# Two decode layers over a KV cache: layer 1's loop behind the kept heads, one K tile loaded in between, their results copied by ScalarE

## The chip, the cores and the metric

The kernel runs on one core of one Trainium2 chip. The metric is the device time of one execution in microseconds (us). A core has five engines with a queue each: TensorE (PE; its weight loads are listed as PEld), VectorE (DVE), ScalarE (ACT), GpSimd (POOL) and SyncE (SP), and 16 DMA engines that they share. All data is in HBM at the start; it has to be brought into SBUF, the core's working memory, before an engine can use it. Matrix products land in PSUM.

## The reference

Two equal layers, each an attention block with a KV cache of 16,384 positions, followed by a small mixer and MLP. One new token for each of two batches; 32 heads of width 128, model width 576, MLP width 4608; bf16 inputs.

```python
def _A_ref(x, k_cache, v_cache, wq, wo):
    q = (x @ wq).reshape(B, Sq, H, Dh).transpose(0, 2, 1, 3)
    scores = jnp.einsum("bhqd,bhkd->bhqk", q, k_cache) * (Dh ** -0.5)
    p = _softmax(scores, axis=-1)
    o = jnp.einsum("bhqk,bhkd->bhqd", p, v_cache)
    return o.transpose(0, 2, 1, 3).reshape(B, Sq, H * Dh) @ wo
...
x = x + _A_ref(_layernorm(x), A_k_cache, A_v_cache, A_wq, A_wo)
x = x + _B_ref(_layernorm(x), B_w1, B_w2, B_w3, B_w4)
x = x + _A_ref(_layernorm(x), A_k_cache, A_v_cache, A_wq, A_wo)
x = x + _B_ref(_layernorm(x), B_w1, B_w2, B_w3, B_w4)
```

Both layers read the same caches, 2 x 32 heads with 4.19 MB of K and 4.19 MB of V each, and the same weights.

## The kernel before, in words

**Work and order.** One step of a layer is one (batch, head) with its K tile and V tile, each 128 partitions x 128 rows of 128 numbers. There are U = 64 steps in each layer. Layer 0 takes the heads in order; layer 1 starts with the last three (`order`), whose tiles are still in SBUF when layer 0 ends, so that these need not be loaded again: heads 62 and 63 whole (`CARRY = 2`), of head 61 the K tile and the last 56 of 128 rows of V; the other `GONE = 72` rows give their place to weights and are loaded again in four pieces.

**Memory and loads.** `mem` has six slots of one tile each. `plan_all` writes down by hand the list of all loads with their places; `Store.pump` issues them on SP strictly in that order, each as soon as its place is free. A tile is free when the last instruction that reads it is done, so SP waits for TensorE, VectorE or ScalarE, and behind a waiting load all later loads wait too. In the loops two V tiles of neighbouring heads come as one load of 8.39 MB, a pair (`plan_pair`).

**One step.** Half of a K tile's rows (64 of each partition's 128) go over TensorE: eight chunks, each of eight transposes into PSUM (`transposes`, L1297), an evacuation by ScalarE (`evacuate`, L1313) and eight matmuls with the query (`scores`, L1327). The other half goes over VectorE: four times a product with the query copied to all partitions (L1347) and a sum (L1353, `dots`). `q_broadcast` makes the next step's query (L1261 to L1271: two VectorE instructions, one matmul, one ScalarE copy). `softmax_max` takes the maxima on VectorE and the maximum over partitions on GpSimd (L1369); `softmax_exp` is on ScalarE (L1378 to L1384); `pv` is 128 matmuls with V (L1468). In the loops `pv_pair` does two heads with 256 matmuls (L1442), after `spread_p` (L1416, L1422), and ScalarE copies the two results (L1446).

**Loops.** In each layer most steps are a loop of two steps a turn, with the instructions of TensorE, ScalarE and VectorE written once: steps `ENTER` to `LEAVE`, 1 to 61 in layer 0 and 4 to 62 in layer 1. What stands ahead of the loop and behind it is straight code. GpSimd has no loop: it tells the looped engines of each tile that has landed (`landed`, a wait and an increment in GpSimd's order) and does the maxima in between.

**Between the layers.** Behind layer 0's attention come the projections with wo, w3 and w4, then wq for layer 1. The weights pass through small places in slots 1 and 4. TensorE meanwhile transposes the kept heads' other half (`turn`), since layer 1 takes heads 62 and 63 over TensorE alone. `carried` then is steps 0, 1 and 2 of layer 1, written out by hand: scores of both kept heads (`still`), the rest of head 61's K (`fresh`, `third`, `dots`), and the three softmaxes and V products. Step 3 (and, behind the loop, steps 62 and 63) run in the same straight loop body as in layer 0. In the version before, step 3 stands between `carried` and the loop, and the V product of step 2 runs inside it.

**Results.** Each head's output column goes to `o_acc` and its sum to `l`: for steps outside the loops by VectorE (`keep_o`, `keep_l`), inside by ScalarE.

Of the kernel before, what the change touches and what calls it, by code (L numbers as in the profile page):

```python
# [328 lines left out]
class KB:  # L329
# [183 lines left out]
    def plan_all(self):  # L513
# [37 lines left out]

        first = self.order(1)[self.CARRY + 1]
# [6 lines left out]
        assert a == self.CARRY + 2 and z == U - 2  # L559
# [10 lines left out]
        self.cuts["wo", 1] = [(i, j, 3 * T + i * row) for i, j in ((0, 11), (11, 22), (22, 32))]  # L570
        at = 3 * T + 32 * row
        ats = [at, at + w3r, at + 2 * w3r, T, T + w3r]
        assert at + 3 * w3r <= 5 * T
        w4_at = T + w3r + w3r // 2
        self.cuts["w4", 1] = [(a, b, w4_at + a * row) for a, b in ((0, 8), (8, 16))] + \
                             [(a, b, 5 * T + (a - 16) * row) for a, b in ((16, 26), (26, 30), (30, 34), (34, 36))]
        w1_at = 5 * T + 20 * row
        assert w4_at + 16 * row <= 2 * T and w1_at + 5 * row <= 6 * T
        self.plan_rows("wo", 1, self.wo, self.cuts["wo", 1])
# [394 lines left out]
    def attention(self, l):  # L974
# [11 lines left out]
        for s in range(self.CARRY + 1 if l else 0, U):  # L986
# [11 lines left out]
            if s == enter + 1:  # L998
                self.pool(lambda e: e.memset(self.both[64:, 0, :], 0.0), writes=[*self.both_keys, "cleared"])
            after = self.early(l, s - 1)  # L1000
            for c in range(2 * n):
# [16 lines left out]
                if after:  # L1018
                    if c == 2:
                        self.softmax_max(l, s - 1, o[s - 1])  # L1020
                        self.keep_o(l, s - 2)
                        self.keep_l(l, s - 2)
                        self.softmax_exp(l, s - 1, o[s - 1])
                        self.landed(l, "v", o[s - 1])
                    if c in (4, 5):
                        self.pv(l, s - 1, o[s - 1], 2 * c - 8)
                        self.pv(l, s - 1, o[s - 1], 2 * c - 7)
                elif turning:
# [11 lines left out]
                if s >= leave:  # L1040
                    if c == n and still and s == U - self.CARRY:
                        self.unturned = [(v, b) for v in o[U - self.CARRY:] for h in range(2)
                                         for b in range(h * self.BP + self.PB, (h + 1) * self.BP, self.CH)]
                        self.unsettled, self.full = [], ()
                    if c == n and still and (s < U - 1):
                        self.turn(4)
                    if s > leave and (l or s < U - 1):
                        if c == n:
                            self.softmax_exp(l, s - 1, o[s - 1])
                            if l == 0 and s == U - self.CARRY:  # L1050
                                self.store.carve(("v", o[s - 1], 0, self.NB), [self.GONE // 4 * i for i in (1, 2, 3, 4)])
                            self.landed(l, "v", o[s - 1])
                        if 0 <= c - n < 4:
                            self.pv(l, s - 1, o[s - 1], c - n)
            if turning:
# [11 lines left out]
            elif s == enter - 1:  # L1067
                while pend:
                    self.scores(*pend.pop(0))
                self.softmax_max(l, s, u)  # L1070
                if s - 1 >= 0:
                    self.keep_o(l, s - 1)
                    self.keep_l(l, s - 1)
                self.softmax_exp(l, s, u)
                self.landed(l, "v", u)
                self.keep_pair_l(l, s)
                for g in range(4):
                    self.pv(l, s, u, g)
                at = self.place(l, s)
                self.act(lambda e, at=at: e.activation(out=self.o_acc[:, at:at + 1], in_=self.mps[:, 448:449], func=ACT.Copy),  # L1080
                         reads=["ops"], writes=["o_acc"])
        if l == 0:
# [75 lines left out]
    def carried(self, o):  # L1158
# [31 lines left out]
        still(1, 0, N)  # L1190
        self.q_broadcast(o[3], 3)
        self.softmax_exp(1, 0, o[0])
# [65 lines left out]

    def q_broadcast(self, u, s):
        i = self.ix(self.l_now, s)  # L1260
        self.dv(lambda e, c: e.tensor_copy(out=self.q_col[:, i:i + 1], in_=self.q_f[:, bass.ds(c, 1)]),  # L1261
                reads=["q_f"], writes=[("q_col", i)], sig=("qc", i), col=u)
# [4 lines left out]
        qps = self.sps[i][:, 256:384]  # L1267
        self.pe(lambda pe: pe.matmul(qps, lhsT=self.ones_bf[:, :], rhs=self.diag[:, :],  # L1268
                                     start=True, stop=True, skip_group_check=True),
                reads=["ones_bf", "diag"], writes=[("qps", i)], sig=("q", i))  # L1270
        self.act(lambda e: e.activation(out=self.qb[i][:, :], in_=qps, func=ACT.Copy),  # L1271
                 reads=[("qps", i)], writes=[("qb", i)], sig=("qb", i))

# [115 lines left out]
    def keep_o(self, l, s):  # L1389

        self.dv(lambda e, c: e.tensor_copy(out=self.o_acc[:, bass.ds(c, 1)], in_=self.mps[:, 448:449]),
                reads=["ops"], writes=["o_acc"], sig="keep_o", col=self.place(l, s))

# [31 lines left out]
    def keep_pair_l(self, l, s):  # L1425
# [4 lines left out]
                 reads=[("ls0", i), ("ls1", i)], writes=["l"], sig=("keep_l", i), col=self.place(l, s))  # L1430

    def pv_pair(self, l, s, u):

# [16 lines left out]
    def pv(self, l, s, u, g):  # L1450
# [12 lines left out]
        def f(pe):  # L1463
            for b0, m, _, buf, _ in runs:
                for j in range(m):
                    b = b0 + j
                    col = self.column(l, s, b)
                    ins = pe.matmul(self.mps[:, 448:449], lhsT=buf[:, j * 128:(j + 1) * 128], rhs=p[:, col:col + 1],  # L1468
                                    start=b == 0, stop=b == self.NB - 1, skip_group_check=True)
# [98 lines left out]
```

## Time and profile before

| | |
|---|---|
| median of 3 runs | 2552.99 us (2551.66 to 2553.33) |
| profiled execution: its own time | 2552.08 us |
| profiled execution: span from first to last instruction | 2550.1 us |
| mean granted TensorE clock | 0.619 |
| busy: PE, DVE, ACT, POOL | 1588.0, 1875.4, 1250.1, 106.0 us |
| DMA queue of the loads | 1092.39 MB, 99.7% of 16 engines' span |

A busy time says how long an engine was occupied, not whether anyone waited for it. Where an instruction's row ends in brackets, its engine stood idle before it for so many us, and what the brackets name ended that; "issue" is time in which the engine waited for nothing that the profile shows. Rows of SP are the issues of loads, not the loads themselves: "x2" holds two issues, the first at the start and the second at the end of the time given. Line numbers are those of the version before.

### The profile page before, as it was taken

How to read it: one execution, taken by the hardware profiler on the slowest of the kernel's cores; microseconds unless marked ns; L12 is line 12 of the kernel's file. 1: busy time of each engine (PE TensorE's matmuls, PEld its weight loads, DVE VectorE, ACT ScalarE, POOL GpSimd, SP SyncE). 2: the span in 40 equal slices, each digit the busy share in tenths (PEclk: the TensorE clock that was granted, in tenths of full speed). 3: DMA queues.
4: the chain of work that ended last, by engine and by line, in shares of the span. 5: the costliest groups of instructions: out<-in, count | busy, mean ns of one | idle time of the engine just before them, and what ended most of it. 6: DMA issues, size and time to landing. Idle time of an engine off the chain costs nothing.

```text
span 2550.1 us, 75502 instructions
## 1 busy us (share of the span) xinstructions
PE 1588.0 (62%) x34642; PEld 1521.6 (60%) x34642; DVE 1875.4 (74%) x1815; ACT 1250.1 (49%) x2110; POOL 106.0 (4%) x154
## 2 busy tenths in 40 slices
PE   4556666566566566566776666566566566665666
PEld 3556656566565565565766566565565565565665
DVE  5787787777877877877748777877877877777775
ACT  3454555554554544544534544544544545555543
POOL 0000000000000000000000000000000000000000
PEclk8666566665656666665656666665665666656655
DMA  9999999999999999999999999999999999999999
GB/s 411 428 435 432 430 437 431 431 438 429 432 436 428 432 438 428 434 435 428 412 415 389 419 435 431 433 435 429 435 436 428 440 432 427 434 438 426 432 432 395
DMA packets 38431, 1093.18 MB, mean 429 GB/s; under 512 B 4196, under 2 KB 5352, under 8 KB 11496
## 3 DMA queue, kind: packets, MB, share of 16 engines
q1 hardware_dynamic: 38376, 1092.39, 99.7%
q8 instruction: 41, 0.67, 0.1%
q14 instruction: 14, 0.11, 0.0%
HBM read 1092.37 MB, written 0.00 MB: 428 GB/s over the span
## 4 chain that ended last, share of the span: by engine, by line
DMA 59%; DVE 26%; PE 7%; issue 5%; ACT 2%; SPq 0%; POOL 0%; POOLq 0%; DVEq 0%; ACTq 0%
DMA mem<-in_A_k_cache_dram 57%; DVE s_dve L1353 16%; DVE prod L1347 9%; PE tps L1297 3%; DMA mem<-in_B_w_dram 1%; PE mps L1468 1%; PE sps L1327 1%; PE mps L1442 1%; ACT kt L1313 1%; PE sps L1268 1%; SPq L101 0%; ACT mem L1313 0%; DVE diag L1264 0%; DVE q_col L1261 0%; DMA mem<-in_A_wq_dram 0%
## 5 line engine op out<-in xcount | busy, mean ns | idle before, releaser
L1353 DVE TENSOR_REDUCE s_dve<-prod 128x16 f32<-128x2048 bf16 x504 | 1151.2, 2284 | 13.2
L1313 ACT ACTIVATE kt<-tps 128x1024 bf16<-128x1024 bf16 x992 | 965.9, 1029 | 183.2 <-PE tps L1297 172.0
L1347 DVE TENSOR_TENSOR prod<-mem,qb 128x2048 bf16<-128x2048 bf16 x492 | 602.2, 1224 | 533.3 <-POOLq L202 482.9
L1297 PE MATMUL tps<-same,mem 128*128 128x128 bf16 x8192 | 911.4, 285 | 34.0 <-issue 26.4
L1297 PEld LDWEIGHTS tps<-same,mem 128*128 128x128 bf16 x8192 | 732.2, 131 | 40.1 <-issue 32.3
L1442 PEld LDWEIGHTS mps<-both,mem 128*128 128x128 bf16 x15104 | 407.6, 103 | 47.6 <-ACT both L1422 43.3
L1442 PE MATMUL mps<-both,mem 128*128 128x2 bf16 x15104 | 412.6, 165 | 32.0 <-ACT both L1422 27.8
L1327 PE MATMUL sps<-q_col,kt 128*128 128x1 bf16 x7936 | 364.2, 168 | 50.5 <-ACT kt L1313 45.2
L1327 PEld LDWEIGHTS sps<-q_col,kt 128*128 128x128 bf16 x7936 | 351.9, 108 | 69.4 <-ACT kt L1313 67.1
L1416 PE MATMUL sps<-p,same 128*128 128x128 bf16 x236 | 46.6, 301 | 484.3 <-ACT p L1384 484.3
L1416 PEld LDWEIGHTS sps<-p,same 128*128 128x128 bf16 x236 | 15.5, 110 | 494.3 <-ACT p L1384 494.3
L1268 PE MATMUL sps<-diag,same 128*128 128x128 bf16 x126 | 36.1, 286 | 286.6 <-DVE diag L1264 281.3
L1369 POOL PARTITION_ALL_REDUCE mx<-mx x128 | 102.9, 804 | 2374.6 <-DVE mx L1367 2257.1
L1446 ACT ACTIVATE o_acc<-mps 128x2 f32 x59 | 10.2, 173 | 382.9 <-PE mps L1442 382.9
L1378 ACT ACTIVATE mx<-mx 128x1 f32<-128x1 f32 x128 | 26.0, 203 | 337.7 <-POOL mx L1369 337.7
L1268 PEld LDWEIGHTS sps<-diag,same 128*128 128x128 bf16 x126 | 13.2, 105 | 296.6 <-DVE diag L1264 296.6
L1271 ACT ACTIVATE qb<-sps 128x128 bf16<-128x128 f32 x123 | 33.9, 275 | 219.6 <-PE sps L1268 219.6
L1422 ACT ACTIVATE both<-sps 64x256 bf16<-64x256 f32 x118 | 44.5, 378 | 57.5 <-PE sps L1416 57.5
L1364 DVE TENSOR_REDUCE mx<-sps 128x1 f32<-128x64 f32 x128 | 28.2, 220 | 24.9 <-PE sps L1327 24.8
L1381 ACT ACTIVATE p<-s_dve,mx 128x64 bf16<-128x64 f32 x123 | 42.8, 348 | 4.0
L1313 ACT ACTIVATE mem<-tps 128x1024 bf16<-128x1024 bf16 x32 | 31.6, 1030 | 20.9 <-PE tps L1297 18.0
L1428 ACT ACTIVATE l<-ls 128x1 f32 (+1 forms) x120 | 35.4, 295 | 9.2
(131 smaller groups left out, 460.6 us busy)
## 6 DMA issues: line engine op xcount, KB each, us to landing
mem<-in_A_k_cache_dram SPq DMA_DIRECT2D x124, 4096.0 KB, 24.6
mem<-in_A_v_cache_dram SPq DMA_DIRECT2D x5, 4096.0 KB, 32.0
mem<-in_B_w_dram SPq DMA_DIRECT2D x21, 576.0 KB, 8.0
mem<-in_B_w_dram SPq DMA_DIRECT2D x7, 1152.0 KB, 40.9
mem<-in_A_v_cache_dram SPq DMA_DIRECT2D x3, 2048.0 KB, 39.0
mem<-in_A_wq_dram SPq DMA_DIRECT2D x10, 512.0 KB, 7.0
mem<-in_A_wo_dram SPq DMA_DIRECT2D x8, 576.0 KB, 16.4
mem<-in_A_wq_dram SPq DMA_DIRECT2D x4, 1024.0 KB, 8.1
```

What stands on the lines that cost most here:

```text
L1268: self.pe(lambda pe: pe.matmul(qps, lhsT=self.ones_bf[:, :], rhs=self.diag[:, :], start=True, stop=True, skip_group_check=True), reads=["o ...
L1297: ins = pe.transpose(self.tps[t][:, j * 128:(j + 1) * 128], buf[:, j * 128:(j + 1) * 128], self.ident[:, :])
L1313: self.act(lambda e: e.activation(out=out, in_=self.tps[t][:, :], func=ACT.Copy), reads=[("tps", t)], writes=keys, sig=("evac", c, t, k))
L1327: ins = pe.matmul(self.sps[sp][:, c * self.CH + j:c * self.CH + j + 1], lhsT=buf[:, j * 128:(j + 1) * 128], rhs=self.q_col[:, sp:sp + 1], ...
L1347: self.dv(lambda e: e.tensor_tensor(out=prod, in0=buf.rearrange("p (j d) -> p j d", d=128), in1=qbc, op=ALU.mult), reads=[("qb", r)] + key ...
L1353: self.dv(lambda e: e.tensor_reduce(out=sd[:, c0:c0 + DB], in_=prod, axis=AX.X, op=ALU.add), reads=["prod"], writes=[("s_dve", r)], sig=(" ...
L1369: self.pool(lambda e: e.partition_all_reduce(mx[3], mx[2], channels=128, reduce_op=ROP.max), reads=[("mx2", i), "cleared"], writes=[("mx3" ...
L1381: self.act(lambda e: e.activation(out=p[:, n:self.NB], in_=self.s_dve[i][:, 0:self.NB - n], func=ACT.Exp, bias=mx[4], scale=self.scale, ac ...
L1416: ins = pe.matmul(out[:, h * n:(h + 1) * n], lhsT=lhsT, rhs=self.p[i][:, :], start=True, stop=True, skip_group_check=True)
L1422: self.act(lambda e: e.activation(out=self.both[lo:hi, k, :], in_=out[lo:hi, :], func=ACT.Copy), reads=[("sps", 0), ("qps", 0)], writes=se ...
L1428: self.act(lambda e, c: e.activation(out=self.l[:, bass.ds(c, 1)], in_=self.ls[:, 0, i:i + 1], func=ACT.Identity, bias=self.ls[:, 1, i:i + ...
L1442: ins = pe.matmul(self.mps[:, 448:450], lhsT=buf[:, b * 128:(b + 1) * 128], rhs=self.both[:, :, col], start=b == 0, stop=b == 2 * self.NB ...
```

## The change

The loop of layer 1 takes steps 3 to 61 instead of 4 to 62, so that `carried` is directly followed by the loop, and three steps instead of two come behind it. The places in `mem` and the order of loads change with it: K of step 3 comes in four pieces into slot 3, K of step 4 into slot 5, then K of step 61, one of the last heads, into slot 0, where it stays until the loop is over; pairs go to slots 1 and 2. V of step 3 is loaded as half of a pair. In `carried` the V products come one after the other instead of in halves between the chunks, step 2's as well, and `keep_by_act` lets ScalarE copy the three results. Step 3's query is spread through PSUM bank 0. Behind the loops, `softmax_max` of the step before stands one chunk earlier, ahead of the second of VectorE's four products, and `softmax_exp` stands at chunk 2 instead of chunk 4; in layer 0 the four transposes of `turn(4)`, which stood at chunk 4, come behind all chunks of step 62.

```diff
-    ENTER = (1, 4)
-    LEAVE = (61, 62)
+    ENTER = (1, 3)
+    LEAVE = (61, 61)
...
-        for i in (1, 2, 3, None, 0):
-            if i is None:
-                self.plan_piece("k", first, T, self.rows_of("k", first), 0, quarter)
-            else:
-                self.plan_piece("v", third, 4 * T, self.rows_of("v", third), i * self.GONE // 4, self.GONE // 4)
+        for i in (1, 2, 3, 0):
+            self.plan_piece("v", third, 4 * T, self.rows_of("v", third), i * self.GONE // 4, self.GONE // 4)
...
-        self.plan_tile("k", first, 3, (quarter, half, half + quarter), quarter)
-        self.plan_tile("v", first, 5)
         for s in range(a, z, 2):
-            self.plan_tile("k", o[s], 0)
-            self.plan_tile("k", o[s + 1], 2)
-            self.plan_pair(o[s], 3)
-        self.plan_tile("k", o[z], 1)
-        self.plan_tile("k", o[z + 1], 5)
-        self.plan_tile("v", o[z], 0)
-        self.plan_tile("v", o[z + 1], 2, (half,))
+            self.plan_tile("k", o[s], 3, (quarter, half, half + quarter) if s == a else ())
+            self.plan_tile("k", o[s + 1], 5)
+            if s == a:
+                self.plan_tile("k", o[z], 0)
+            self.plan_pair(o[s], 1)
+        self.plan_tile("k", o[z + 1], 4)
+        self.plan_tile("k", o[z + 2], 3)
+        self.plan_tile("v", o[z], 5)
+        self.plan_tile("v", o[z + 1], 1)
+        self.plan_tile("v", o[z + 2], 2, (half,))
...
                 elif s > leave:
-                    if c == LEAD:
+                    if c == LEAD - 1:
                         self.softmax_max(l, s - 1, o[s - 1])
...
-                    if c == n and still and (s < U - 1):
-                        self.turn(4)
-                    if s > leave and (l or s < U - 1):
-                        if c == n:
-                            self.softmax_exp(l, s - 1, o[s - 1])
...
+                if s > leave and (l or s < U - 1):
+                    if c == LEAD:
+                        self.softmax_exp(l, s - 1, o[s - 1])
...
+            if still and s == U - self.CARRY:
...
+                self.turn(4)
...
-        self.q_broadcast(o[3], 3)
+        self.q_broadcast(o[3], 3, 0)
...
-        for g in range(2):
+        for g in range(4):
             self.pv(1, 0, o[0], g)
+        self.keep_by_act(1, 0)
         third(3)
         fresh(5)
-        for g in range(2, 4):
-            self.pv(1, 0, o[0], g)
         third(4)
         fresh(6)
+        dots(2)
         self.softmax_exp(1, 1, o[1])
-        dots(2)
-        self.keep_o(1, 0)
-        self.keep_l(1, 0)
         third(5)
         fresh(7)
-        for g in range(2):
-            self.pv(1, 1, o[1], g)
         third(6)
-        for g in range(2, 4):
-            self.pv(1, 1, o[1], g)
         third(7)
         dots(3)
+        self.softmax_max(1, 2, o[2])
+        for g in range(4):
+            self.pv(1, 1, o[1], g)
+        self.softmax_exp(1, 2, o[2])
+        self.keep_by_act(1, 1)
+        self.landed(1, "v", o[2])
+        for g in range(4):
+            self.pv(1, 2, o[2], g)
+        self.keep_by_act(1, 2)
...
+    def keep_by_act(self, l, s):
+
+        i, c, k = self.ix(l, s), self.place(l, s), 448
+        self.act(lambda e: e.activation(out=self.o_acc[:, c:c + 1], in_=self.mps[:, k:k + 1], func=ACT.Copy),
+                 reads=["ops"], writes=["o_acc"])
+        if self.columns(l, s) == self.NB:
+            self.act(lambda e: e.activation(out=self.l[:, c:c + 1], in_=self.ls[:, 0, i:i + 1], func=ACT.Copy),
+                     reads=[("ls0", i)], writes=["l"])
+        else:
+            self.keep_pair_l(l, s)
```

The last weights of layer 1 move to other slots with the tiles: wo to slots 4 and 5, w3 to slots 4, 5 and 0, w4 to slots 0 and 3, w1 to slot 3 (before: 3 and 4; 3, 4 and 1; 1 and 5; 5).

More of the change, by code (lines that the diff above doesn't have):

```diff
@@ new lines, in plan_all @@
+            self.plan_pair(o[s], 1)
[4 more added lines that the diff above has]
+        self.plan_tile("v", o[z + 2], 2, (half,))
+        self.cuts["wo", 1] = [(i, j, 4 * T + i * row) for i, j in ((0, 11), (11, 22), (22, 32))]
+        at = 4 * T + 32 * row
+        ats = [at, at + w3r, at + 2 * w3r, 0, w3r]
+        assert at + 3 * w3r <= 6 * T
+        w4_at = w3r + w3r // 2
@@ L575, in plan_all @@
         self.cuts["w4", 1] = [(a, b, w4_at + a * row) for a, b in ((0, 8), (8, 16))] + \
-                             [(a, b, 5 * T + (a - 16) * row) for a, b in ((16, 26), (26, 30), (30, 34), (34, 36))]
-        w1_at = 5 * T + 20 * row
-        assert w4_at + 16 * row <= 2 * T and w1_at + 5 * row <= 6 * T
+                             [(a, b, 3 * T + (a - 16) * row) for a, b in ((16, 26), (26, 30), (30, 34), (34, 36))]
+        w1_at = 3 * T + 20 * row
+        assert w4_at + 16 * row <= T and w1_at + 5 * row <= 4 * T
@@ L1039, in attention @@
                             self.keep_l(l, s - 2)
[L1040 to L1044, printed above, removed]
-                    if c == n and still and (s < U - 1):
-                        self.turn(4)
-                    if s > leave and (l or s < U - 1):
-                        if c == n:
[L1049 to L1054, printed above, removed]
+                if s > leave and (l or s < U - 1):
+                    if c == LEAD:
+                        self.softmax_exp(l, s - 1, o[s - 1])
+                        if l == 0:
+                            self.store.carve(("v", o[s - 1], 0, self.NB), [self.GONE // 4 * i for i in (1, 2, 3, 4)])
+                        self.landed(l, "v", o[s - 1])
+                    if 0 <= c - n < 4:
+                        self.pv(l, s - 1, o[s - 1], c - n)
+            if still and s == U - self.CARRY:
+                self.unturned = [(v, b) for v in o[U - self.CARRY:] for h in range(2)
+                                 for b in range(h * self.BP + self.PB, (h + 1) * self.BP, self.CH)]
+                self.unsettled, self.full = [], ()
+                self.turn(4)
             if turning:
@@ L1389, in keep_o @@
     def keep_o(self, l, s):
-        self.dv(lambda e, c: e.tensor_copy(out=self.o_acc[:, bass.ds(c, 1)], in_=self.mps[:, 448:449]),
-                reads=["ops"], writes=["o_acc"], sig="keep_o", col=self.place(l, s))
+        k, c = 448, self.place(l, s)
+        self.dv(lambda e: e.tensor_copy(out=self.o_acc[:, c:c + 1], in_=self.mps[:, k:k + 1]),
+                reads=["ops"], writes=["o_acc"])
     def keep_l(self, l, s):
```

41 lines of the change are left out of this document (11 added, 30 removed).

## The prediction

> **What bounds the kernel now.** I read the page first, then the windows (columns: busy us of PE, PEld, DVE, ACT, POOL; PEclk; DMA share; GB/s), then the timelines of single engines around the places that the change touches.
>
> ```profile
> span 2550.1 us, 75502 instructions
> HBM read 1092.37 MB, written 0.00 MB: 428 GB/s over the span
> DMA 59%; DVE 26%; PE 7%; issue 5%; ACT 2%; SPq 0%; POOL 0%; POOLq 0%; DVEq 0%; ACTq 0%
> 1525.00:2378.14 853.14, 530.23 (x11399) 509.69 (x11398) 644.31 (x573) 427.90 (x727) 35.27 (x44) 0.62 1.00 433
> 1370.00:1412.00 42.00, 29.14 (x650) 26.21 (x648) 32.49 (x28) 25.58 (x42) 1.60 (x2) 0.75 0.85 346
> ```
>
> The kernel is a stream of 1092 MB. In the loop the DMA share is 1.00 at 433 GB/s, so a 4.19 MB tile takes 9.7 us and a turn of four tiles 38.8 us, and no engine is busy for more than 644 of 853 us. The change leaves the bytes as they are, so it can only win where the stream runs dry, or lose where it makes it dry. The second window is the one dry place of any size: (433 − 346) / 433 × 42 us = 8.4 us, right behind the entry into layer 1's loop. That is the ceiling of the gain. Finer windows and the issues on SP show why:
>
> ```profile
> 1382.00:1384.00 2.00, 0.50 (x5) 0.50 (x6) 1.97 (x2) 1.00 (x6) 0.45 (x1) 0.50 1.06 459
> 1384.00:1386.00 2.00, 2.00 (x32) 1.92 (x29) 1.97 (x5) 1.48 (x3) 0.00 (x0) 0.50 0.42 180
> 1386.00:1388.00 2.00, 1.54 (x26) 1.44 (x25) 2.00 (x2) 1.77 (x3) 0.00 (x0) 0.69 0.00 0
> 1388.00:1390.00 2.00, 0.35 (x8) 0.27 (x8) 1.07 (x5) 0.63 (x3) 0.35 (x1) 1.00 1.04 270
> 1398.00:1400.00 2.00, 0.34 (x13) 0.28 (x11) 1.97 (x2) 0.00 (x0) 0.00 (x0) 0.50 0.21 82
> 1400.00:1402.00 2.00, 1.36 (x17) 1.27 (x17) 1.97 (x5) 0.17 (x1) 0.00 (x0) 0.50 1.11 360
> 1402.00:1404.00 2.00, 2.00 (x27) 2.00 (x26) 2.00 (x1) 1.96 (x3) 0.00 (x0) 0.50 0.46 164
> 1321.75 0.33 SPq L101 DMA_DIRECT2D mem<-in_A_v_cache_dram  x1
> 1329.41 10.80 SPq L101 DMA_DIRECT2D mem<-in_A_k_cache_dram  x2
> 1353.02 0.33 SPq L101 DMA_DIRECT2D mem<-in_A_v_cache_dram  x1
> 1372.85 14.95 SPq L101 DMA_DIRECT2D mem<-in_A_k_cache_dram  x2
> 1400.76 0.33 SPq L101 DMA_DIRECT2D mem<-in_A_v_cache_dram  x1
> ```
>
> The row 1372.85 holds two issues, the second at its end, 1387.5. The queue empties at 1384.9 (180 of 433 GB/s in that slice), because the K tile of 1372.85 is the last that was issued; the next comes at 1387.5 and moves data from 1388.75 (270 of 433), 1.3 us after the issue. It is alone again, the queue empties at 1398.4, and the pair of V tiles of 1400.76 flows only from 1403. Two gaps of 3.9 and 3.8 us make nearly all of the 8.4.
>
> **1: the order of the loads.** K(n) and V(n) are the tiles of step n of layer 1. What has moved when the queue empties at 1384.9, counted from the issue of 1321.75, is V(3), K(4), K(5), the V pair of 4 and 5 (two tiles), K(6): six tiles. In the changed order the same places hold K(4), K(61), the pair of 3 and 4, K(5), K(6): six tiles as well. K(4) waits for the same scores as V(3) did, and K(61) for the end of step 0's product with V, as K(4) did. The pair waits for the end of step 1's product with V: at 1340, worked out in 2, while data is queued to 1346.1 (1384.9 less the last four tiles, 38.8). So the new stream is full up to 1384.9 too, if K(5) and K(6) are issued in time, and the next thing that it then needs is the second pair, where the old one needed a K tile. Step 3's query goes through bank 0 with the same four instructions: 0.
>
> **2: when TensorE reaches the loop.** Those three issues hang on the loop's first turn, so on its first transposes.
>
> ```profile
> 1319.48 2.24 PE L1327 MATMUL sps<-q_col,mem 128*128 128x1 bf16 x78 [1.47 <-issue]
> 1322.80 0.83 PE L1468 MATMUL mps<-both,mem 128*128 128x1 bf16 x25 [0.33 <-ACT both L1384]
> 1325.40 1.20 PE L1468 MATMUL mps<-both,mem 128*128 128x1 bf16 x39 [1.78 <-issue]
> 1332.15 0.93 PE L1297 MATMUL tps<-same,mem 128*128 128x128 bf16 x7 [2.43 <-issue]
> 1338.86 0.99 PE L1468 MATMUL mps<-p,mem 128*128 128x1 bf16 x32 [1.16 <-issue]
> 1351.63 0.29 PE L1297 MATMUL tps<-same,mem 128*128 128x128 bf16 x1 [1.42 <-issue]
> 1354.11 0.38 PE L1327 MATMUL sps<-q_col,kt 128*128 128x1 bf16 x8 [0.70 <-ACT kt L1313]
> 1356.44 3.57 PE L1468 MATMUL mps<-both,mem 128*128 128x1 bf16 x128 [1.95 <-ACT both L1384]
> 1365.68 2.74 PE L1297 MATMUL tps<-same,mem 128*128 128x128 bf16 x24 [5.67 <-issue]
> 1391.54 6.80 PE L1442 MATMUL mps<-both,mem 128*128 128x2 bf16 x249 [0.47 <-ACT both L1422]
> 1400.13 0.33 PE L1442 MATMUL mps<-both,mem 128*128 128x2 bf16 x7 [1.79 <-issue]
> ```
>
> In the straight code TensorE stops after every 128 matmuls (78 + 1 + 24 + 25 from 1319.48 to the stop before 1325.40; then 128 and 127) with no releaser, and the blocks start 5.9, 6.75 and 6.7 us apart, although a block of 128 alone takes 3.57. At the jump into the loop it stands for 5.67. I read both as the fetch of instructions behind the data. The change takes out of this stretch step 3's 64 transposes, 64 scores and 128 V matmuls, and puts the kept heads' V matmuls one after the other. From 1319.48 there remain 78 + 1 + 24 + 128 (V of step 0) + 64 (the rest of K(2)) + 2 × 128 (V of 1 and 2) = 551 matmuls, four blocks and 39. The first blocks start as before, at 1319.48, 1325.40, 1332.15 and 1338.86, the last at 1338.86 + 6.7 = 1345.6. Inside them step 1's V matmuls end 39 matmuls after 1338.86, at 1340 (the pair's issue of 1), and step 2's 39 after 1345.6, at 1346.7 (39 took 1.20 at 1325.40). With 5.67 for the jump the loop begins at 1352.4 instead of 1365.68. Bounds: 1344 without the stops (a rival, below), 1356 if each of three fetches is 1 us later.
>
> [...]
>
> **3: the first turn.** Measured from its first transposes at 1365.68, the old turn issued its K tiles at +7.2 and +21.8 and the pair at +35.1 (1.79 of it the stop at 1400.13). Its first K tile had landed and its VectorE half was done ahead in both versions; afterwards the turn is bound by its own chain, so I keep the offsets. New issues: 1359.6, 1374.2, 1387.5. Data for the first two must be there when the tiles before them are through, at 1365.5 and 1375.2 (1384.9 less two tiles and one): with the 1.3 us of start the first makes it, and the second is 0.3 late, which the next gap is then shorter by. The pair does not: dry from 1384.9 to 1387.5 + 1.3 = 1388.8, 3.9 us. Behind the pair I take the old course, without a further gap. So one gap of two is left: the gain is the second, 3.8 us, up to 4.5 if the slices around the first (0.8 us of the 8.4 lie before it) recover too. In general the loss is (entry + 36.4 − 1384.9), against 8.4 now, once the entry is later than 1348.5.
>
> **4: results on ScalarE.** Two small VectorE copies for each kept head go, and two ScalarE activations come, each behind its head's V matmuls. ScalarE then holds evacuation 5 of K(2) behind step 0's V matmuls, but TensorE makes its transposes only after them; and step 2's V matmuls wait for the copy of step 1's result, 0.3 us. Both lie inside the blocks of 2: 0. If the fetch were no cover they would cost those 0.3 us each.
>
> **5: exp in layer 0's end.** ScalarE now takes the exp of layer 0's step 61 behind chunk 2 of step 62, before four evacuations are queued behind it, and the four extra transposes move behind the chunks.
>
> ```profile
> 1230.20 1.22 DVE L1347 TENSOR_TENSOR prod<-mem,qb 128x2048 bf16<-128x2048 bf16 x1
> 1233.67 0.21 DVE L1362 TENSOR_REDUCE mx<-s_dve 128x1 f32<-128x64 f32 x1
> 1234.29 1.25 POOL L1369 PARTITION_ALL_REDUCE mx<-mx  x1 [30.12 <-DVE mx L1367]
> 1235.58 0.20 ACT L1378 ACTIVATE mx<-mx 128x1 f32<-128x1 f32 x1
> 1244.79 7.74 ACT L1313 ACTIVATE mem<-tps 128x1024 bf16<-128x1024 bf16 x8 [1.43 <-PE tps L1297]
> 1265.67 2.05 PE L1297 MATMUL tps<-same,mem 128*128 128x128 bf16 x16
> ```
>
> The maximum is queued one product and sum earlier on VectorE (1233.67 − 1230.20 = 3.5 us), so the exp comes at 1234.29 − 3.5 + 1.25 = 1232.0 instead of 1235.58, and ScalarE stands some 2 us for it; the V matmuls are 3 us earlier, but the moved transposes come after them, and the run of eight evacuations starts at 1245.1 instead of 1244.79. The layer's end, whose first use of wo (just before 1265.67) lets the weight loads go on, moves by +0.3 us; bounds −0.5 and +1.5, the wait in ScalarE being the later end. Cost +0.3.
>
> **6: three heads behind the loop.** The stream's last tiles are in the same number, so all of the tail shifts with the stream; what can be added is the compute.
>
> ```profile
> 2480.74 1.23 DVE L1347 TENSOR_TENSOR prod<-mem,qb 128x2048 bf16<-128x2048 bf16 x1 [7.75 <-DMA mem<-in_A_k_cache_dram]
> 2509.81 0.22 DVE L1362 TENSOR_REDUCE mx<-s_dve 128x1 f32<-128x64 f32 x1
> 2512.65 0.23 DVE L1364 TENSOR_REDUCE mx<-sps 128x1 f32<-128x64 f32 x1 [2.61 <-PE sps L1327]
> 2543.18 2.11 PE L897 MATMUL mps<-prod,mem 128*128 128x2 bf16 x70 [1.63 <-DMA mem<-in_B_w_dram]
> 2546.04 1.15 PE L897 MATMUL mps<-prod,mem 128*128 128x2 bf16 x30 [0.76 <-DMA mem<-in_B_w_dram]
> ```
>
> The loop ends one tile, 9.7 us, earlier on the stream's clock, and VectorE finds K(61) landed: it starts at 2480.74 − 7.75 − 9.7 = 2463.3, where it now stands for 7.75 us. Three heads at (2509.81 − 2480.74) / 2 = 14.5 end at 2506.9; two waits of 2.5 to 3 us for scores of TensorE, which leaves the loop later and holds its V matmuls of step 61 until V(61) lands, at some 2490, bring the last maximum to about 2513 against 2512.65. The weights' last matmuls wait for DMA (1.63 + 0.76, and 0.6 between), 3.0 us of cover. So 0; bounds 0 and +1.5. The last weights now lie where K(63) is: their place comes free at the same point of the last step as before.
>
> **Sum.** −3.8 + 0.3 + 0 = −3.5, on the profiled execution's 2552.08; the median of the runs is 2552.99, 0.9 above it and within their spread of 1.7. From the median: 2549.5.
>
> **Rivals.** *The stops go.* With no fetch to wait for, the matmuls from 1322.80 take three times 3.57, 2.74 for three groups of transposes (the row at 1365.68), 1.15 for 40 scores (78 took 2.24) and 1.2 for one wait for an evacuation and one hand-off (0.70 and 0.47): 1338.6, and the loop begins at 1344. The pair is issued at 1379, both gaps go: −8.4 + 0.3, 2544.9. For it: from 1338.86 to the stop before 1351.63 TensorE passed 256 matmuls, so one boundary unseen, though it waited for others there. Against it: four stops in a row where the matmuls are dense. An entry before 1351.5 is enough for over 5 us, and my 1352.4 is near it. Chance 0.34. *The entry is no earlier* (slower). If the fetches, in a stream that no longer pauses, cost so much more that the loop still begins at 1365.68, all three issues come late: dry 8.6, 4.9 and 3.6 us, 17.1 against 8.4, +8.7 and 0.3: 2562. It decides from an entry at 1357 on, where the new gaps equal the old. Against it: the slowest spacing shown is 6.75. Chance 0.08, and 0.03 more for a tail that uses up its 3 us and more. The forecast itself, one gap left: 0.55, own range 2547 to 2552.5.
>
> **How the numbers follow.** 0.2% (5.1 us) is about what a measurement of this kernel can tell from no change. The faster rival is over it, the forecast within it with 0.01 of its edge beyond, and the slower ones beyond it but for 0.01. Range: from 0.6 below the faster rival to an entry at 1357 with 1.5 for the layer's end (2552.99 − 8.4 + 8.5 + 1.5): 2544.3 to 2554.6.
>
> **What would show it.** Right: TensorE's first block in the loop at 1351 to 1354 after a stop of 5 to 6 us; one slice of 0 GB/s near 1387 and none near 1400; the tail's last matmuls still waiting for weights. Wrong: no dry slice (first rival), two or three (second), or wo's matmuls starting over 3 us later against the last V tile than now.

## The result and the profile after

| | before | changed |
|---|---|---|
| median, 20 runs each | 2553.11 us (2551.66 to 2557.31) | 2549.10 us (2547.98 to 2552.14) |
| ratio, 95% interval | | 0.9985 (0.9978 to 0.9992) |
| profiled execution: own time, span | 2552.08, 2550.1 us | 2549.13, 2547.4 us |

The changed kernel is 4.0 us (0.15%) faster; 2549.5 was forecast. Line numbers are now those of each kernel itself: transposes L1278 (L1297 before), V products L1462 (L1468), pair products L1435 (L1442), wo and w4 L894 (L897).

The page and the windows of the changed kernel, with the columns of before:

```profile
HBM read 1092.37 MB, written 0.00 MB: 429 GB/s over the span
```
```profile
1260.00:1320.00 60.00, 45.09 (x1103) 42.52 (x1101) 17.33 (x82) 19.90 (x24) 0.35 (x1) 0.50 1.00 393
1370.00:1412.00 42.00, 26.21 (x577) 23.86 (x575) 33.43 (x33) 22.99 (x42) 1.96 (x3) 0.62 0.96 402
1384.00:1386.00 2.00, 0.00 (x0) 0.00 (x0) 1.97 (x2) 0.00 (x0) 0.00 (x0) 0.50 0.60 246
1386.00:1388.00 2.00, 1.36 (x17) 1.28 (x17) 1.97 (x2) 0.17 (x1) 0.00 (x0) 0.50 1.34 442
1388.00:1390.00 2.00, 2.00 (x28) 2.00 (x26) 1.97 (x2) 1.96 (x3) 0.00 (x0) 0.50 0.26 98
1400.00:1402.00 2.00, 0.00 (x0) 0.00 (x0) 2.00 (x3) 0.23 (x1) 0.00 (x0) 0.56 1.21 524
1525.00:2378.14 853.14, 529.83 (x11398) 509.31 (x11396) 644.32 (x573) 427.86 (x727) 35.33 (x44) 0.62 1.00 433
2510.00:2540.00 30.00, 19.31 (x502) 18.55 (x499) 9.65 (x55) 4.79 (x8) 0.00 (x0) 0.50 1.01 415
2540.00:2552.00 12.00, 4.87 (x130) 4.17 (x130) 0.66 (x3) 1.02 (x4) 0.00 (x0) 0.61 0.24 85
```

The loop runs at 433 GB/s as before. The dry place lost (433 − 346) / 433 × 42 = 8.4 us before and loses (433 − 402) / 433 × 42 = 3.0 now. The gap near 1400 has gone: 524 where 360 stood. The one near 1385 is left in part, without a slice at 0. A slice of 2 us can hold packets that reach past its end (one shows 524 GB/s), so how the 3.0 us lie between 1384 and 1390 is not readable. The edges of the wide window have the same flaw: with its end at 1470 the two kernels differ by 5.6 us, with its end at 1525 by 4.5, where these 42 us show 5.4. The trace's DMA records, with each packet spread over the time it took, give 7.8 us lost before and 3.2 now in the same 42 us, and 4.5 between the two whichever of these ends is taken. So 4.5 us came back.

SP's issues and TensorE's blocks of the changed kernel, from its timelines:

```profile
1338.86 0.33 SPq L101 DMA_DIRECT2D mem<-in_A_v_cache_dram  x1
1358.14 14.95 SPq L101 DMA_DIRECT2D mem<-in_A_k_cache_dram  x2
1386.77 0.33 SPq L101 DMA_DIRECT2D mem<-in_A_v_cache_dram  x1
```
```profile
1324.34 2.91 PE L1462 MATMUL mps<-both,mem 128*128 128x1 bf16 x104 [1.23 <-issue]
1331.08 1.01 PE L1278 MATMUL tps<-same,mem 128*128 128x128 bf16 x8 [2.55 <-issue]
1343.76 1.23 PE L1462 MATMUL mps<-p,mem 128*128 128x1 bf16 x40 [2.16 <-issue]
1350.85 2.74 PE L1278 MATMUL tps<-same,mem 128*128 128x128 bf16 x24 [5.87 <-issue]
1386.13 0.33 PE L1435 MATMUL mps<-both,mem 128*128 128x2 bf16 x7 [2.48 <-issue]
```

Three of the four stops stand where they were forecast, 1 to 2 us earlier; the one forecast for 1338.86 did not come. The loop begins at 1350.85 (forecast 1352.4) behind a jump of 5.87 us. The K tiles are issued at 1358.14 and 1372.8 (the row holds both), the pair at 1386.77.

### The profile page after: what moved, and what is told of

The parts are those of the page before. It is cut to its first block, busy times and chain, and to the rows that moved or that the text cites. A ratio compares the mean times of both kernels' runs of the same rounds, so it can differ in the third digit from the quotient of the medians.

```text
span 2547.4 us, 75501 instructions
## 1 busy us (share of the span) xinstructions
PE 1588.6 (62%) x34642; PEld 1521.1 (60%) x34642; DVE 1875.5 (74%) x1811; ACT 1250.6 (49%) x2114; POOL 106.2 (4%) x154
## 4 chain that ended last, share of the span: by engine, by line
DMA 59%; DVE 27%; PE 7%; issue 5%; ACT 1%; POOL 0%; SPq 0%; POOLq 0%; DVEq 0%; ACTq 0%
DMA mem<-in_A_k_cache_dram 56%; DVE s_dve L1334 17%; DVE prod L1328 9%; PE tps L1278 3%; DMA mem<-in_B_w_dram 1%; DMA mem<-in_A_v_cache_dram 1%; PE mps L1462 1%; PE sps L1308 1%; PE sps L1249 1%; PE mps L1435 1%; ACT mem L1294 0%; DVE diag L1245 0%; PE mps L894 0%; ACT kt L1294 0%; DVE q_col L1242 0%
## 5 line engine op out<-in xcount | busy, mean ns | idle before, releaser
L1278 PE MATMUL tps<-same,mem 128*128 128x128 bf16 x8192 | 910.7, 285 | 32.4 <-issue 25.7
L1278 PEld LDWEIGHTS tps<-same,mem 128*128 128x128 bf16 x8192 | 732.0, 131 | 38.2 <-issue 31.3
L1435 PEld LDWEIGHTS mps<-both,mem 128*128 128x128 bf16 x15104 | 407.5, 103 | 48.6 <-ACT both L1404 43.4
L1435 PE MATMUL mps<-both,mem 128*128 128x2 bf16 x15104 | 412.6, 165 | 33.0 <-ACT both L1404 27.8
```

The costliest lines, as they stand in the source:

```text
L1278: ins = pe.transpose(self.tps[t][:, j * 128:(j + 1) * 128], buf[:, j * 128:(j + 1) * 128], self.ident[:, :])
L1435: ins = pe.matmul(self.mps[:, 448:450], lhsT=buf[:, b * 128:(b + 1) * 128], rhs=self.both[:, :, col], start=b == 0, stop=b == 2 * self.NB ...
```

## The experiments

Each kernel was run beside the kernel before, so times are best read as distances to it within a session (e1 to e4, e5 to e8 and e9 to e11 are three sessions):

| run | what it is | median, us | to before | ratio, 95% interval |
|---|---|---|---|---|
| e1 | changed, K of step 62 early | 2548.20 | −4.8 | 0.9983 (0.9974 to 0.9992) |
| e2 | changed, K of step 61 late | 2555.31 | +2.3 | 1.0010 (1.0001 to 1.0019) |
| e3 | changed, one V product twice | 2556.03 | +3.0 | 1.0014 (1.0005 to 1.0023) |
| e4 | changed, results on VectorE | 2550.14 | −2.9 | 0.9989 (0.9980 to 0.9998) |
| e5 | changed, half of K of step 62 early | 2546.61 | −5.9 | 0.9978 (0.9969 to 0.9987) |
| e6 | changed, queue emptied ahead of the loop | 2560.49 | one run | |
| e7, e10 | changed, layer 0's exp undone | 2550.42, 2550.16 | −2.1, −2.3 | 0.9991 (0.9982 to 1.0000), 0.9990 (0.9981 to 0.9999) |
| e8, e11 | changed, unaltered | 2548.42, 2549.03 | −4.1, −3.4 | 0.9985 (0.9976 to 0.9994), 0.9987 (0.9978 to 0.9996) |
| e9 | before, with layer 0's exp alone | 2552.42 | 0.0 | 0.9999 (0.9990 to 1.0008) |

### Is it the entry into the loop? (e3)

```diff
-        for g in range(4):
-            self.pv(1, 2, o[2], g)
+        for again in (True, False):
+            for g in range(4):
+                self.pv(1, 2, o[2], g, again)
...
```

> The 128 matmuls of step 2's product with V are issued twice (the second time starts the sums anew). Theory (in this stretch TensorE is paced by the fetch of its instructions, 6.7 us for 128 matmuls): the loop begins 6.7 us later, 1357.5, and as the loss is the entry + 36.4 - 1384.9, all of it is lost: 2555.8. Rival 1 (the stops are waits that the extra work would fill, 3.57 us for 128 matmuls): entry 1354.4, 2552.7. Rival 2 (the gap is not set by the entry): 2549.

TensorE, SP and two windows of this kernel:

```profile
1343.49 3.58 PE L1463 MATMUL mps<-p,mem 128*128 128x1 bf16 x128 [2.42 <-issue]
1350.50 1.22 PE L1463 MATMUL mps<-p,mem 128*128 128x1 bf16 x40 [3.44 <-issue]
1357.94 2.74 PE L1279 MATMUL tps<-same,mem 128*128 128x128 bf16 x24 [6.21 <-issue]
1393.21 0.33 SPq L101 DMA_DIRECT2D mem<-in_A_v_cache_dram  x1
```
```profile
1340.00:1370.00 30.00, 17.34 (x402) 16.16 (x398) 14.03 (x11) 11.30 (x15) 0.00 (x0) 0.61 0.98 410
1370.00:1412.00 42.00, 23.91 (x527) 22.07 (x527) 35.91 (x33) 21.57 (x41) 2.86 (x3) 0.67 0.86 357
```

128 matmuls more, which alone take 3.58, put the entry from 1350.85 to 1357.94: 7.1 us, one block more, 7.0 us behind the one at 1343.49. The loss is (433 − 410) / 433 × 30 + (433 − 357) / 433 × 42 = 9.0 against 9.4 by entry + 36.4 − 1384.9, and the time is 6.9 above the changed kernel's 2549.1 (6.7 expected). Both rivals are out.

### Is the fetch slow because of the data? (e6)

```diff
             self.plan_tile("k", o[s], 3, (quarter, half, half + quarter) if s == a else ())
-            self.plan_tile("k", o[s + 1], 5)
             if s == a:
-                self.plan_tile("k", o[z], 0)
+                self.plan_tile("k", o[z], 4)
+            self.plan_tile("k", o[s + 1], 5)
...
-        self.plan_tile("k", o[z + 1], 4)
+        self.plan_tile("k", o[z + 1], 0)
```

> K of step 61 is loaded into the slot that V of step 2 leaves, and ahead of K(4), so all loads behind K(3) wait for the end of step 2's product with V and the queue stands empty from some 1329 on. Theory (the fetch of TensorE's instructions is slow because it runs behind the data): from then on the stops of 2.16 to 2.55 us after 128 matmuls shrink to under 0.7, the last product with V ends near 1341.5 instead of 1345.0, and the loop begins at 1344 to 1347. Time: dry from 1328.5 to 1342.8 (14.3) instead of 3.0: near 2560. Rival (a block of instructions takes its 6.7 us whatever the queue does): stops as before, products end at 1345.0, the loop begins at 1350.9; dry to 1346.3: 2564.

Window and TensorE of this kernel:

```profile
1320.00:1340.00 20.00, 16.24 (x505) 15.53 (x502) 17.50 (x16) 7.62 (x21) 1.60 (x2) 0.50 0.34 137
```
```profile
1332.72 3.55 PE L1462 MATMUL mps<-p,mem 128*128 128x1 bf16 x128
1336.62 3.55 PE L1462 MATMUL mps<-p,mem 128*128 128x1 bf16 x128 [0.35 <-ACT l L1420]
1341.79 2.74 PE L1278 MATMUL tps<-same,mem 128*128 128x128 bf16 x24 [1.61 <-issue]
```

With the queue empty (137 GB/s over 20 us) the stops are gone altogether: where the changed kernel stands for 2.55 us at 1331.08 and 2.16 at 1343.76, nothing stands here, two V products run through at 3.55 us each, and the jump into the loop costs 1.61 instead of 5.87. The loop begins at 1341.79, earlier than the theory's 1344 to 1347. So it is the stream of loads that brings the stops, and the rival of a fixed 6.7 us falls. The time fits: 13.7 us are lost in this window and 1.0 in the next 30 us (419 GB/s), but only 0.3 of the 3.0 us behind the entry (430 GB/s), which makes 11.5; the profiled execution is 11.4 us longer than that of the changed kernel.

That the stops are a fetch of instructions can be read from the trace too. The profile's page lists a DMA queue of instructions (packets, MB, share), here of the changed kernel and of e3:

```profile
q8 instruction: 41, 0.67, 0.1%
```
```profile
q8 instruction: 42, 0.69, 0.1%
```

e3's 128 matmuls more are one packet more. In the trace's DMA records of the changed kernel such packets start at 1328.61, 1341.24 and 1348.36, each takes 1.0 to 1.1 us, and TensorE goes on 1.4 to 1.5 us after each has landed (1331.08, 1343.76 and, behind the jump, 1350.85). In that kernel they start 6.2 to 7.1 us apart. In e6 they start at 1322.59, 1325.92 and 1329.40, 3.3 and 3.5 us apart as the queue drains, and take 0.9 to 1.5 us. So the packet itself is not slower beside the data; it comes later. What holds it up until then no record shows.

### Is it the tile in between? (e2)

```diff
-            if s == a:
-                self.plan_tile("k", o[z], 0)
             self.plan_pair(o[s], 1)
+        self.plan_tile("k", o[z], 0)
         self.plan_tile("k", o[z + 1], 4)
```

> The K tile of step 61 is loaded behind the loop instead of in between. Theory: the queue holds a tile less. Dry from 1338.2 (K(4) landed) to the pair's issue at 1338.9 plus 1.3: 1.9 us; K(5) in time; K(6), issued at 1372.8, is needed at 1369.2: 4.9 us; the second pair, issued at 1386.8, is needed at 1383.8: 4.3 us. Sum 11.1 against 3.0 now: 2549.1 + 8 = 2557, later than the kernel before. Rival (the direct entry into the loop alone brings the gain, the load in between is hidden anyway): 2549 to 2550.

Windows and TensorE of this kernel:

```profile
1320.00:1340.00 20.00, 13.96 (x418) 13.30 (x416) 15.71 (x14) 7.62 (x21) 1.91 (x3) 0.50 0.93 379
1340.00:1370.00 30.00, 17.01 (x319) 15.41 (x316) 24.22 (x23) 17.12 (x26) 1.25 (x1) 0.70 0.95 401
1370.00:1412.00 42.00, 27.88 (x686) 25.53 (x686) 29.42 (x27) 20.72 (x41) 1.96 (x3) 0.64 0.92 389
```
```profile
1338.00 3.55 PE L1461 MATMUL mps<-p,mem 128*128 128x1 bf16 x128 [0.35 <-ACT l L1419]
1346.78 2.74 PE L1277 MATMUL tps<-same,mem 128*128 128x128 bf16 x24 [5.23 <-issue]
```

Lost are 2.5 + 2.2 + 4.3 = 9.0 us against 11.1 expected and 3.2 in the changed kernel's same three windows, and the kernel is slower than the one before: the tile in between is what makes the early entry pay. The expected 2557 was 1.7 us too high; it held the entry at 1350.85, and the entry came at 1346.78. The queue was empty near 1337 (8 GB/s between 1336 and 1338), and there a fetch went through: two instruction packets start 3.6 us apart (1333.99 and 1337.55), and the 128 matmuls at 1338.00 run in one piece. Of the 4.1 us by which the loop begins earlier, 1.1 were there before (this product starts at 1338.00, in the changed kernel at 1339.11).

### Who copies the results? (e4)

```diff
-        self.keep_by_act(1, 0)
+        self.keep_o(1, 0)
+        self.keep_l(1, 0)
...
-        self.keep_by_act(1, 2)
+        self.keep_o(1, 2)
+        self.keep_l(1, 2)
```

(The same for head 1.)

> The three kept heads' results are copied by VectorE (a copy of o and one of l, or a sum) instead of ScalarE. The prediction put this part at 0. By the trace of the changed kernel: VectorE's copy of step 2's result waits for the end of its matmuls, so VectorE's first product in the loop starts at 1345.3 instead of 1336.1; it now stands 8.35 us before 1358.8 for the broadcast query, so step 4's first product starts at 1359.8 instead of 1358.8 and the second pair is issued 1 us later: 2550.1. Rival (the waiting copy holds the whole first turn back): 9 us later, 2558. Rival (0 as predicted): 2549.1.

VectorE, TensorE and SP of this kernel:

```profile
1344.95 0.16 DVE L1376 COPY o_acc<-mps 128x1 f32<-128x1 f32 x1 [5.99 <-PE mps L1465]
1345.66 1.22 DVE L1331 TENSOR_TENSOR prod<-mem,qb 128x2048 bf16<-128x2048 bf16 x1 [0.48 <-issue]
1350.86 2.74 PE L1281 MATMUL tps<-same,mem 128*128 128x128 bf16 x24 [5.95 <-issue]
1387.95 0.33 SPq L101 DMA_DIRECT2D mem<-in_A_v_cache_dram  x1
```

VectorE stood 5.99 us for a copy of one column and entered the loop at 1345.66. The entry of TensorE was the same (1350.86), but the pair was issued at 1387.95 instead of 1386.77: 1.2 us, and the distance to before shrank by 1.1. Time alone could not tell that from nothing; the issue time can.

### Layer 0's exp (e7, e9, e10; e8 and e11 beside them)

```diff
-                    if c == LEAD - 1:
+                    if c == (LEAD - 1 if l else LEAD):
                         self.softmax_max(l, s - 1, o[s - 1])
...
-                    if c == LEAD:
+                    if c == (LEAD if l else n):
                         self.softmax_exp(l, s - 1, o[s - 1])
```

(And `turn(4)` back to chunk 4; e9 is the opposite edit in the kernel before.)

> The layer 0 part alone is undone: maximum, exp and the four extra transposes of step 62 stand where they stood before. Theory: exp of step 61 at 1235.6 instead of 1231.7, the run of evacuations ends at 1252.5 instead of 1252.0, layer 0 ends 0.2 to 0.5 us later: 2549.1 + 0.3. Rival (this part brings the gain): 2552 to 2553.

> The changed kernel once more, unaltered, on the same chip as the runs beside it: 2549.1, so that the half tile and the old exp are compared within one session.

> The kernel before with the layer 0 part of the change alone (maximum, exp and the four extra transposes of step 62). With that part undone the changed kernel took 2550.4 instead of 2548.4. Theory: the part brings 0.8 us in the layer's end (the loads of wo there are issued at 1264.5 in the traces with it, at 1265.3 and 1265.7 without) and no more: 2552.5 - 0.8 = 2551.7. Rival (it brings the 2.0 us of that pair of medians): 2550.5. Prediction on record: +0.3, 2552.8.

> The changed kernel with the layer 0 part undone, once more, beside the changed kernel: theory 0.8 us above it, rival 2.0 us above it, prediction on record 0.3 below it.

> The changed kernel once more, unaltered, for the two beside it: 2548.4 to 2549.1.

First the changed kernel's ScalarE; then, each with TensorE at the loop and the dry window, the changed kernel in e8 and the one with the exp undone in e10:

```profile
1231.69 0.20 ACT L1359 ACTIVATE mx<-mx 128x1 f32<-128x1 f32 x1 [1.97 <-POOL mx L1350]
1240.90 11.11 ACT L1294 ACTIVATE mem<-tps 128x1024 bf16<-128x1024 bf16 x12 [1.42 <-PE tps L1278]
```
```profile
1348.23 2.74 PE L1278 MATMUL tps<-same,mem 128*128 128x128 bf16 x24 [5.39 <-issue]
```
```profile
1370.00:1412.00 42.00, 26.53 (x612) 24.51 (x610) 30.66 (x30) 21.79 (x42) 1.96 (x3) 0.62 0.99 423
```
```profile
1354.37 2.74 PE L1278 MATMUL tps<-same,mem 128*128 128x128 bf16 x24 [6.85 <-issue]
```
```profile
1370.00:1412.00 42.00, 26.99 (x577) 24.71 (x577) 35.82 (x32) 22.95 (x43) 2.77 (x3) 0.66 0.92 387
```

Undoing the part costs 2.0 us in one session and 1.1 in the other, where the two sets of runs overlap (2547.5 to 2553.0 against 2547.8 to 2551.7), so it brings something like 1 to 2. Put alone into the kernel before it brings nothing that shows (2552.42 against 2552.43, where 0.8 was expected). Why is not shown. With the old exp the entries into the loop are 1351.24 (e7) and 1354.37 (e10), with the new one 1350.85, 1348.23 (e8) and 1350.54 (e11); but the entries of e1 and e5 below, with the new exp, are 1353.66 and 1353.18, so the entry alone does not tell the two apart. In e9 the loop begins at 1365.78, as in the kernel before (1365.68). The stream differs already ahead of the entry: between 1260 and 1320 it moved 386 and 380 GB/s with the old exp in the changed kernel, and 390 to 400 in nine executions of it and its variants with the new one; in the kernel before it was 398, and 397 in e9. Two executions with the old exp are few.

Single executions of the two kernels show what goes with the entry (the losses are those of the windows, at 433 GB/s):

| kernel | lost in 1260 to 1320 | entry | lost in 1370 to 1412 | entry + 36.4 − 1384.9 | own time |
|---|---|---|---|---|---|
| changed (e8) | 5.3 | 1348.23 | 1.0 | −0.3 | 2546.06 |
| changed (e11) | 5.4 | 1350.54 | 2.3 | 2.0 | 2547.79 |
| changed | 5.5 | 1350.85 | 3.0 | 2.4 | 2549.13 |
| exp undone (e7) | 6.5 | 1351.24 | 3.1 | 2.7 | 2550.34 |
| exp undone (e10) | 7.3 | 1354.37 | 4.5 | 5.9 | 2551.98 |

From the first row to the last the gap behind the entry grows by 3.5 us and the loss ahead of it by 2.0, together 5.5 of the 5.9 us between the times. So the entry is not all that differs between executions.

### Filling the rest of the gap (e1, e5)

```diff
             self.plan_pair(o[s], 1)
-        self.plan_tile("k", o[z + 1], 4)
+            if s == a:
+                self.plan_tile("k", o[z + 1], 4)
```

> One more K tile (that of step 62) is loaded ahead of the loop, into the slot that step 2's V tile leaves, behind the first pair; it is taken out of the end. Theory (the queue runs dry where an issue comes later than the data queued): the queue then holds data to 1384.9 + 9.7 = 1394.6, and the second pair is issued at 1386.8 as before, so the 3.0 us lost between 1370 and 1412 go (433 GB/s there) and the whole stream moves up: 2549.1 - 2.6 to 3.0 = 2546.3. Rival (the end is set by the compute behind the loop, not by the stream): 433 GB/s there too, but the time stays at 2549 and the last matmuls no longer wait for weights. Second rival (the loop needs this tile's place in the order at its end): a dry slice near 2440 to 2480, time 2549 or more.

Here the dry window, VectorE's first product behind the loop, and TensorE at the end:

```profile
1370.00:1412.00 42.00, 23.64 (x518) 22.35 (x518) 28.32 (x25) 19.31 (x33) 0.90 (x2) 0.62 1.02 438
```
```profile
2467.97 1.22 DVE L1329 TENSOR_TENSOR prod<-mem,qb 128x2048 bf16<-128x2048 bf16 x1
2520.16 3.12 PE L895 MATMUL mps<-prod,mem 128*128 128x2 bf16 x111 [0.32 <-DVE prod L1100]
2543.91 0.59 PE L895 MATMUL mps<-prod,mem 128*128 128x2 bf16 x16 [0.30 <-issue]
```

The gap has gone (438), but only 0.8 us came of it (−4.8 to before, against the −4.0 of the result). The loop now lags the stream by a tile more: VectorE begins the three last heads at 2467.97 (2458.84 in the changed kernel), wo begins at 2520.16 (2514.96), and the last matmuls wait for no weights. That is the first rival: the compute behind the loop takes the gain. So half a tile should do both:

```diff
+            if s == a:
+                self.plan_piece("k", o[z + 1], 4 * T, self.rows_of("k", o[z + 1]), 0, half)
-        self.plan_tile("k", o[z + 1], 4)
+        self.plan_piece("k", o[z + 1], 4 * T, self.rows_of("k", o[z + 1]), half, half)
```

> As the run in which step 62's K tile was loaded early, but only its first half (2.1 MB, 4.85 us) goes behind the first pair; the second half stays behind the loop. There the gap had gone (438 GB/s between 1370 and 1412) but the loop ran a whole tile later against the stream, and the output projection of the last layer began at 2520.2 instead of 2515.0: the compute behind the loop had eaten the gain (2548.2). Theory: the half covers the gap of 3.0 us, and the compute comes 4.85 instead of 9.7 us later, with 5.2 us of waits for weights (0.76 + 1.56 + 2.20 + 0.70) to take it: 2549.1 - 2.6 = 2546.5, and the last matmuls still wait a little for weights. Rival (the early tile brought so little because the stream lost the time elsewhere): 2548 to 2549 again.

The dry window and TensorE's last weights of this kernel:

```profile
1370.00:1412.00 42.00, 27.52 (x582) 25.74 (x583) 35.17 (x32) 23.43 (x43) 1.60 (x2) 0.62 1.00 426
```
```profile
2537.53 2.03 PE L896 MATMUL mps<-prod,mem 128*128 128x2 bf16 x70 [2.08 <-DMA mem<-in_B_w_dram]
2540.36 1.22 PE L896 MATMUL mps<-prod,mem 128*128 128x2 bf16 x30 [0.80 <-DMA mem<-in_B_w_dram]
```

0.7 us is lost in the window, the last matmuls wait for weights again, and the median is 2546.61: 5.9 below the kernel before, and 1.8 below the changed kernel in the same session (2.6 expected). It is the fastest version here, though its interval overlaps that of the changed kernel.

## Why the prediction was right, step by step

**1, order of loads.** Right. The pair was issued at 1338.86 (1340), and the queue ran out near 1385.1 (246 of 433 in the slice from 1384). What was needed next was the pair. e2 and e6 bear out the counting of tiles within 1.5 us: by the DMA records their last data landed at 1336.8 and 1328.7, where 1338.2 and 1328.5 were expected.

**2, entry.** Right in mechanism (e3, e6), 1.5 us late in size. The last block stood at 1343.76 instead of 1345.6. Of these 1.8 us, 1.1 are that the stretch began earlier in this execution (1324.34 against 1325.40 for the second block). The rest goes with the fourth stop, which did not come: its boundary lies inside the 128 matmuls that start at 1334.94 and took 3.82 us in one row, against 3.55 to 3.58 alone. TensorE reached it near 1337.4 (88 matmuls take 2.49), and an instruction packet had landed at 1336.07. In other executions TensorE does stop there, 0.68 us in e11 and 1.55 in e10. The entry of the unaltered changed kernel scatters from 1348.2 to 1350.9, which the prediction, from one execution of before, could not see.

**3, first turn.** The offsets held: +7.3, +21.9 and +35.9 against +7.2, +21.8 and +35.1, the last because the stop in the pair's product took 2.48 instead of 1.79. One gap of two went, and of the other 3.0 us were left where 3.9 were forecast; the slice at 0 GB/s, one of the signs of being right, did not come. The term was mis-sized: 4.5 us came back where 3.8 stood, the upper bound that was given. The pair's issue came 0.7 us before the forecast 1387.5, with the entry 1.5 earlier and the offset 0.8 longer, and that is the difference. The faster rival differs from the forecast only in the entry. Its condition, an entry before 1351.5, was met by 0.65 us (1350.85) without its cause, the missing stops. e8's profiled execution, at 1348.23 and 2546.06 us, came close to its time, with three of the stops still there (1.50, 2.28 and 1.88 us).

**4, results on ScalarE.** Put at 0 as two exchanged copies, with VectorE's place in the queue left out. On VectorE they hold the loop's products back by 9.6 us, of which 1.2 reaches the pair (e4). Against the kernel before the term can still be near 0, since there no copy stood in that place; no run tests that.

**5, exp in layer 0.** The times were right (exp at 1231.69 against 1232.0), the sign was not: the run of evacuations does not begin at 1245.1 but joins the four in front of it, twelve from 1240.90 to 1252.0, so it ends 0.5 us earlier than before (eight from 1244.79 to 1252.5) instead of 0.3 later. The part as a whole is worth some 1 to 2 us in the changed kernel (e7, e10), against a cost of 0.3; how so much comes of it stays open.

**6, the tail.** TensorE of before where wo begins, with two windows of before, and VectorE and TensorE of the changed kernel:

```profile
2520.75 3.15 PE L897 MATMUL mps<-prod,mem 128*128 128x2 bf16 x112 [0.32 <-DVE prod L1121]
```
```profile
2510.00:2540.00 30.00, 21.25 (x569) 20.49 (x567) 9.12 (x53) 6.60 (x13) 0.35 (x1) 0.50 1.01 417
2540.00:2552.00 12.00, 6.47 (x175) 5.71 (x171) 1.88 (x11) 2.45 (x6) 0.00 (x0) 0.50 0.58 222
```
```profile
2458.84 1.22 DVE L1328 TENSOR_TENSOR prod<-mem,qb 128x2048 bf16<-128x2048 bf16 x1
2514.96 3.12 PE L894 MATMUL mps<-prod,mem 128*128 128x2 bf16 x111 [0.32 <-DVE prod L1099]
2540.20 2.30 PE L894 MATMUL mps<-prod,mem 128*128 128x2 bf16 x70 [2.20 <-DMA mem<-in_B_w_dram]
2543.21 1.25 PE L894 MATMUL mps<-prod,mem 128*128 128x2 bf16 x30 [0.70 <-DMA mem<-in_B_w_dram]
```

VectorE starts the three heads at 2458.84 (2463.3 less the stream's 4 us: 2459.3), wo begins 5.8 us earlier than before (2520.75), and the last matmuls wait longer for weights. The compute takes nothing, as said; e8's execution, further ahead on the stream, ended 3.1 us earlier still. VectorE waited once for scores (3.83 us) where two waits were forecast, and its last maximum came at 2506.9, some 2 us ahead of the forecast 2513 less the stream's 4. What the earlier maximum and exp do behind layer 1's loop no run tells apart.

**The sum.** In the two profiled executions the gap gave 4.5, but the span fell by 2.7 only. 0.7 us went in a slower stretch between 1260 and 1320 (393 against 398 GB/s), nearly all of it from 1300 on (384 against 400), where the change reorders layer 1's first loads; e2, with the same order there, moved 399, so the cause is open. About 1.2 was lost among the last weights: from 2510 on the changed kernel moved 415 × 30 + 85 × 12 = 13.5 MB and the one before 15.2 (417 and 222), 3.9 us at 433 GB/s, and ended 2.7 earlier. The matmuls were waiting for weights there, so it is the stream; what slowed it was not traced. Against the forecast −3.5 the profiled execution shows −3.0 and the medians −4.0. That both are near is partly luck: the gap gave 0.7 us more than its term and layer 0's end helped instead of costing 0.3, and the two losses, which were not in the sum, took this back.

## What to carry to other kernels

Where a kernel is one stream, ask for each load what is queued when it is issued: here the change closed 4.5 us of dry time, by early issues and by data put in between (e2 shows that one without the other was slower than before), and the median fell by 4.0. A load brought forward made the loop lag the stream by about its own length (e1: VectorE behind the loop 9.1 us later for a tile of 9.7 us), so bring forward only what the gap needs and the compute behind the loop can bear. Straight code of many small instructions was not free here beside a saturated DMA queue (mostly 5.9 to 7.0 us for 128 matmuls that alone take 3.55): count its blocks, above all ahead of a jump.

## What the runs showed of the hardware that was not expected

The stops of TensorE every 128 matmuls came and went with the loads: up to 3.44 us each with the queue full (e3), though some boundaries were passed in one piece even then (near 1337.4 in the changed kernel), and none with it empty (e6); the jump into the loop took 4.44 (e9) to 6.85 us (e10) against 1.61 in e6. In e2 the empty queue thus repaired part of its own damage: two instruction packets started 3.6 us apart there, against 6.2 to 7.1 in the changed kernel, and the entry came 4.1 us earlier, 3.0 of it from where the queue was empty. And executions of one kernel differ by up to 2.6 us at this entry; the gap behind it then differs by 2.0 (1.0 against 3.0), of the 3.1 us between their times.
